# Per-column weight scales from products on TensorE, and column scales moved into the third stage's split

## The chip, the cores and the metric

The kernel runs on one core of one Trainium2 chip. The metric is the device time of one execution in microseconds (us), lower is better. The engines are named as in the profile: PE multiplies matrices (PEld is its weight load), DVE and ACT work on vectors, POOL is GpSimd, and SP issues nearly all DMAs.

## What is computed

An attention over 4 batches of 12 heads (448 rows, head size 64, RMS-normed q and k) is followed by two MLPs on 1792 tokens. The weights arrive as 64-bit floats.

```
def _moe_ref(x, w_a, w_b, w_out):
    a = x @ w_a
    b = x @ w_b
    return (a * b @ w_out)
def _moe2_ref(x, w_in, w_out, alpha):
    h = x @ w_in
    g = np.maximum(h, 0.0) + alpha * np.minimum(h, 0.0)
    return (g @ w_out)
...
    attn_out = _attn_ref(**attn_kwargs)
    x = np.ascontiguousarray(attn_out.transpose(0, 2, 1, 3)).reshape(B * S, H * D)
    x = _moe_ref(x=x, **moe_kwargs)
    return _moe2_ref(x=x, **moe2_kwargs)
```

Here w_a and w_b are 768 x 1536, the first w_out is 1536 x 768, w_in is 768 x 2048 and the second w_out is 2048 x 768.

## The kernel before

**Precision.** Every 32-bit operand of the four matrix products is written as the sum of two 16-bit halves, after a power-of-two scale that keeps it in range; a product is then three 16-bit matmuls (hi·hi, hi·lo, lo·hi: `prod`). `power` (L111 to L121) turns a sum of squares into the scale `s` and its inverse `i`, with three small DVE operations.

**Stages.** Each batch b passes four stages: a (w_a and w_b, 24 weight units of 6 chunks), y (first w_out, 12 units of 6), h (w_in, 16 units of 6) and o (second w_out, 24 units of 4). They run in the order a0 y0 h0 o0 a1 y1 a2 h1 o1 y2 a3 h2 y3 o2 h3 o3. A unit is 18 matmuls of 448 columns on PE (12 in stage o). Attention runs ahead: batch 0's before a0 (here called the prologue), the other batches' steps between the units of the stages, by the table RATE.

**Weights.** Each of the 76 units is prepared once, for batch 0, in four steps that run ahead of the unit that PE multiplies. `w_load` (10 units ahead) brings the 64-bit numbers into one of 3 `raw` buffers. `w_convert` (8 ahead) makes 32-bit floats `wf`: one ACT operation (L631), two DVE operations (L634, L637), for stage o a third that multiplies the rows by the inverse scales of stage h's columns (L643), and then an ACT Square with a running sum (L653). `w_scale` (6 ahead) sums the squares over the partitions with a matmul against ones (the tile `tot`) and calls `power`. `w_split` (3 ahead) writes the two halves (ACT L686, DVE L687) and stores them in HBM, from where the batches 1 to 3 reload them.

**Around it.** Stage h's output g is `split` with one constant `cg` (L741, L742). Stage o ends for each of 6 column blocks with ACT (L847), four transposes on PE (L854), a DVE operation `ob` that multiplies by the batch's scale `cum` (L856), and the store. A softmax step has DVE operations on the row sums `su` (L441 in batch 0, L467 later, then a reciprocal). `prep1` computes inverse roots with 3 Newton rounds of 3 DVE operations (L261, L262, L265).

**PSUM.** `ps_s` (scores) has 2 buffers of two banks, `ps_m` (tile `p`) has 3 of one bank, and `ps_x` has a single bank (tile tag `x`), which the attention's output product, `tot` and `norm` use in turn.

**Order.** The order of each engine's instructions is set when the program is built: by a scheduler that follows the order of the code as a priority and its own costs. Each engine then runs its list in order.

## Time and profile before

| what | value |
|---|---|
| median of 3 runs | 1286.08 us (1284.34 to 1286.24) |
| the profiled execution's own time | 1286.1 us |
| its span in the trace | 1283.9 us |
| PE busy | 1177.9 us, 92% of the span |
| ACT busy | 734.5 us, 57% |
| DVE busy | 709.6 us, 55% |
| POOL busy | 9.8 us, 1% |

The stretches used below begin at the first matmul of a stage on PE: prologue 0 to 117.6 us, a0 to 231.7, y0 to 294.9, h0 to 362.8, o0 to 466, a1 to 598, y1 to 653.6; then all that is left. The profile is read by these stretches, since a share over the whole span mixes a beginning in which three engines and the DMA share the load with an end in which PE has the work almost alone.

### The profile page before, as it was taken

To read this page: it belongs to the slowest core of one execution; us is meant where nothing else is said; L and a number is where in the kernel's file an instruction comes from. 1 tells how busy PE (TensorE), PEld (TensorE's weight loads), DVE (VectorE), ACT (ScalarE), POOL (GpSimd) and SP (SyncE) were. 2 spreads that over 40 slices of the span, in tenths; PEclk is the share of its full clock that TensorE was granted. 3 is DMA by queue.
4 is the path that set the end of the run, shared out by engine and by line. 5 is a ranking of instruction groups with operands and counts; after the bars stand their busy time and mean duration, and the time that the engine had idled before them with its cause. 6 is when DMAs were issued, how large, how long until landed. Compare 5 with 4: busy or idle time off the path is not lost. (4 is left out here: it accounts for less than half of the span.)

```text
span 1283.9 us, 18197 instructions
## 1 busy us (share of the span) xinstructions
PE 1177.9 (92%) x6574; PEld 604.0 (47%) x6574; DVE 709.6 (55%) x1500; ACT 734.5 (57%) x1480; POOL 9.8 (1%) x32
## 2 busy tenths in 40 slices
PE   6897998888888889887999989999999999999998
PEld 3454544444443444443545545555555555555554
DVE  7988788879897857576545166443111351102410
ACT  7999898999886867577554256544222342212310
POOL 1000000000000000000000000000000000000000
PEclk9998998898998999997999999999999999999999
DMA  6548999999989899986865375687533333344343
GB/s 187 157 156 195 299 295 299 268 296 269 285 220 251 238 235 226 206 210 164 204 153 152 115 169 133 153 189 179 150 112 113 121 112 119 94 137 137 104 124 86
DMA packets 324489, 234.66 MB, mean 183 GB/s; under 512 B 190992, under 2 KB 297744, under 8 KB 324400
## 3 DMA queue, kind: packets, MB, share of 16 engines
q1 hardware_dynamic: 324288, 233.43, 68.9%
q8 instruction: 52, 0.85, 0.3%
q0 software_dynamic: 112, 0.07, 0.1%
q14 instruction: 37, 0.30, 0.1%
HBM read 155.79 MB, written 32.24 MB: 146 GB/s over the span
## 5 line engine op out<-in xcount | busy, mean ns | idle before, releaser
L108 PEld LDWEIGHTS <-w 128*128 128x128 f16 x4896 | 480.2, 100 | 488.8 <-issue 55.5
L108 PE MATMUL p<-x,w 128*128 128x448 f16 x1728 | 339.7, 356 | 10.1 <-ACT t L760 6.7
L108 PE MATMUL p<-g,w 128*128 128x448 f16 x1152 | 232.9, 359 | 9.9 <-DVE w L687 6.9
L108 PE MATMUL p<-y,w 128*128 128x448 f16 x1152 | 225.2, 357 | 0.0
L108 PE MATMUL p<-ab,w 128*128 128x448 f16 x864 | 170.8, 359 | 1.9 <-ACT ab L741 1.9
L108 PE MATMUL s<-kT,qT 128*64 128x448 f16 (+1 forms) x588 | 105.5, 408 | 32.4 <-ACT pf L431 24.7
L414 DVE TENSOR_REDUCE nm<-s 128x2 f32<-128x896 f32 x84 | 91.0, 1084 | 36.2 <-PE s L108 35.9
L475 DVE SCALAR_TENSOR_TENSOR p<-pf,ri,p 128x448 f16<-128x448 f32 x126 | 83.2, 680 | 37.9 <-ACT p L474 37.9
L474 ACT ACTIVATE p<-pf,ri 128x448 f16<-128x448 f32 x126 | 79.9, 662 | 31.9 <-DMA pT<-p 23.5
L431 ACT ACTIVATE pf<-s,nm,esc 128x448 f32<-128x448 f32 x126 | 90.2, 720 | 2.9 <-DVE p L475 1.5
L763 DVE SCALAR_TENSOR_TENSOR ab<-p,inv_a,t 128x448 f32<-128x448 f32 x48 | 32.6, 679 | 100.2 <-PE p L108 99.8
L847 ACT ACTIVATE t<-p,inv_o 128x448 f32<-128x448 f32 x24 | 25.6, 1066 | 102.2 <-PE p L108 102.2
L631 ACT ACTIVATE wf<-raw 128x768 f32<-128x768 f32 (+1 forms) x76 | 63.2, 835 | 28.7 <-DMA raw<-in_moe_w_out_dram 8.8
L856 DVE TENSOR_SCALAR ob<-p,cum 112x512 f32<-112x512 f32 x24 | 18.0, 749 | 107.1 <-PE p L854 56.8
L687 DVE SCALAR_TENSOR_TENSOR w<-wf,sc,w 128x768 f16<-128x768 f32 (+1 forms) x76 | 69.8, 927 | 4.0 <-ACT w L686 3.7
L766 ACT ACTIVATE junk<-ab 128x448 bf16<-128x448 f32 x48 | 27.5, 573 | 74.9 <-DVE ab L763 74.1
L833 DVE SCALAR_TENSOR_TENSOR t<-t,al,p 128x448 f32<-128x448 f32 x64 | 43.4, 679 | 47.6 <-ACT t L832 47.6
L637 DVE SCALAR_TENSOR_TENSOR wf<-raw,wf 128x768 int32<-128x768 int32 (+1 forms) x76 | 65.8, 868 | 0.4
L832 ACT ACTIVATE t<-p 128x448 f32<-128x448 f32 x64 | 34.6, 541 | 54.3 <-PE p L108 54.1
L686 ACT ACTIVATE w<-wf,sc 128x768 f16<-128x768 f32 (+1 forms) x76 | 64.5, 862 | 0.3 <-DVE sc L118 0.3
L653 ACT ACTIVATE junk<-wf 128x768 bf16<-128x768 f32 (+1 forms) x76 | 59.0, 776 | 8.5 <-DVE wf L643 2.9
L741 ACT ACTIVATE g<-t,cg 128x448 f16<-128x448 f32 x64 | 42.6, 666 | 34.7 <-DVE t L833 34.6
(131 smaller groups left out, 1003.3 us busy)
## 6 DMA issues: line engine op xcount, KB each, us to landing
w<-sc_a SPq DMA_DIRECT2D x72, 384.0 KB, 3.2
w<-sc_h SPq DMA_DIRECT2D x48, 384.0 KB, 3.1
w<-sc_o SPq DMA_DIRECT2D x72, 256.0 KB, 3.1
w<-sc_y SPq DMA_DIRECT2D x36, 384.0 KB, 3.2
raw<-in_moe_w_in_dram SPq DMA_DIRECT2D x16, 768.0 KB, 7.0
raw<-in_moe_w_out_dram SPq DMA_DIRECT2D x24, 512.0 KB, 5.0
raw<-in_moe_w_a_dram SPq DMA_DIRECT2D x12, 768.0 KB, 7.2
raw<-in_moe_w_b_dram SPq DMA_DIRECT2D x12, 768.0 KB, 6.0
```

Source lines behind the costliest of these rows:

```text
L108: nc.tensor.matmul(out=o, lhsT=a, rhs=b, start=first, stop=last)
L414: nc.vector.tensor_reduce(out=nm, in_=ps[:, :, 0:S], axis=AX.X, op=ALU.max, negate=True)
L431: nc.scalar.activation(out=pf, in_=ps[:, j, 0:S], func=AF.Exp, bias=nm[:, j:j + 1], scale=scale[j], accum_out=su[:, j:j + 1],)
L474: nc.scalar.activation(out=t[:, 0, :, 0:KP], in_=pf, func=AF.Copy, scale=r)
L475: nc.vector.scalar_tensor_tensor(out=t[:, 1, :, 0:KP], in0=pf, scalar=r, in1=t[:, 0, :, 0:KP], op0=ALU.mult, op1=ALU.subtract,)
L631: nc.scalar.activation(out=t, in_=hi.bitcast(F32), func=AF.Prelu, scale=2.0 ** -112, alpha=-(2.0 ** 32))
L637: nc.vector.scalar_tensor_tensor(out=ti, in0=lo, scalar=29, in1=ti, op0=ALU.logical_shift_right, op1=ALU.bitwise_or)
L653: nc.scalar.activation(out=junk(768, size(kind)), in_=t, func=AF.Square, accum_out=sums[0][:, j:j + 1])
L686: nc.scalar.activation(out=w[:, 0], in_=t, func=AF.Copy, scale=s)
L687: nc.vector.scalar_tensor_tensor(out=w[:, 1], in0=t, scalar=s, in1=w[:, 0], op0=ALU.mult, op1=ALU.subtract)
L741: nc.scalar.activation(out=x[:, 0], in_=t, func=AF.Copy, scale=s)
L833: nc.vector.scalar_tensor_tensor(out=t, in0=t, scalar=al[:, f:f + 1], in1=ps, op0=ALU.mult, op1=ALU.add)
```

## The change

1. `w_gram` takes the place of the Square (L653). For each unit it multiplies the upper 16 bits of `wf` (read as bf16, every second 16-bit element) with themselves on PE: 6 (stage o: 4) matmuls of 128 x 128 into one tile `gram` of `ps_x`. A DVE maximum over its 128 columns gives the bound that the squares gave. It runs 6 units ahead; `w_scale` moves from 6 to 5 ahead.
2. The multiplication of stage o's rows by the inverse scales (L643) goes. `h_scales` folds these scales into a table `cgf`, one column for each f, which the split of g uses in place of `cg`. Until the table is there (in h0), g is kept as 32-bit in `raw`, and is split two at a time afterwards, the rest behind the loop.
3. `ob` moves from DVE to ACT. The third operation of `power`, the operation on `su`, the Newton rounds of all groups from the fourth on (now 4 operations in a round, on DVE as well for the first ones), and two small operations on `al` and `icg` move to POOL. The four operations on `cum` move from the end of stage y to the start of stage o.

```diff
@@ power
-        nc.vector.tensor_scalar(i.bitcast(I32), h, 1.0, float(49 << 23), op0=ALU.mult, op1=ALU.add)
+        nc.gpsimd.tensor_scalar(i.bitcast(I32), h, 1.0, float(49 << 23), op0=ALU.mult, op1=ALU.add)
@@ prep1
+        eng = nc.vector if gs[0] < 3 else nc.gpsimd
         for _ in range(3):
...
+            eng.tensor_tensor(t, r, r, op=ALU.mult)
+            eng.tensor_tensor(t, t, m, op=ALU.mult)
+            eng.tensor_scalar(t, t, -0.5, 1.5, op0=ALU.mult, op1=ALU.add)
+            eng.tensor_tensor(r, r, t, op=ALU.mult)
@@ probs (and the same in probs_f)
-        nc.vector.tensor_scalar(su, su, 1e-9, 2.0 ** -14, op0=ALU.add, op1=ALU.mult)
+        nc.gpsimd.tensor_scalar(su, su, 1e-9, 2.0 ** -14, op0=ALU.add, op1=ALU.mult)
         nc.vector.reciprocal(ri, su)
@@ w_convert, w_gram
-        if kind == "o":
-            k = CHAINS["o"][2]
-            t3 = t.rearrange("p (k f) -> p k f", f=128)
-            nc.vector.tensor_tensor(
...
+    def w_gram(u):
...
+        k = CHAINS[kind][2]
+        tops = wf[u].bitcast(BF16).rearrange("p (k f t) -> p k f t", f=128, t=2)[:, :, :, 1]
+        ps = ps_x.tile([128, 512], F32, tag="x", name="gram")[:, 0:128]
+        for kk in range(k):
+            mm(ps, tops[:, kk], tops[:, kk], kk == 0, kk == k - 1)
+        nc.vector.tensor_reduce(out=sums[0][:, j:j + 1], in_=ps, axis=AX.X, op=ALU.max)
@@ w_scale
+        if (kind, n) == ("h", KF2 - 1):
+            h_scales()
+
+    def h_scales():
+
+        mx = sm_p.tile([128, 1], F32, tag="mh", name="mh")
+        ci = sm_p.tile([128, 1], F32, tag="mh", name="ci")
+        nc.vector.tensor_reduce(out=mx, in_=inv["h"], axis=AX.X, op=ALU.max)
+        nc.vector.tensor_scalar(
+            ci.bitcast(I32), mx.bitcast(I32), -1.0, float(254 << 23), op0=ALU.mult, op1=ALU.add
+        )
+        nc.vector.tensor_scalar(cgf, inv["h"], ci, cg, op0=ALU.mult, op1=ALU.mult)
+        nc.gpsimd.tensor_tensor(icg, icg, mx, op=ALU.mult)
+        state["cgf"] = True
@@ steps
-    STEPS = [(w_load, 10), (w_convert, 8), (w_scale, 6), (w_split, 3)]
+    STEPS = [(w_load, 10), (w_convert, 8), (w_gram, 6), (w_scale, 5), (w_split, 3)]
@@ stage_h
+        def one(f):
+            t = raw.pop(f)
+            G[b, f] = x = slot(f"g{b}_{f}")
+            nc.scalar.activation(out=x[:, 0], in_=t, func=AF.Copy, scale=cgf[:, f:f + 1])
...
-            t = tmp()
+            raw[f] = t = tmp() if state["cgf"] else slot32(f"g32_{b}_{f}")
...
-            G[b, f] = split(t, cg, f"g{b}_{f}")
+            if state["cgf"]:
+                for x in sorted({f, min(raw)}):
+                    one(x)
+        for x in sorted(raw):
+            one(x)
@@ stage_o
-            nc.vector.tensor_scalar(ob, po, cum[:PT, b:b + 1], None, op0=ALU.mult)
+            nc.scalar.activation(out=ob, in_=po, func=AF.Copy, scale=cum[:PT, b:b + 1])
```

Of the 76 units' products, 6 stand in the prologue, 24 in a0, 12 in y0, 16 in h0 (10 of six matmuls, 6 of four) and 18 in o0 (of four). The rest of PE's order is the same in both programs.

On PE at the end of a0, before: two sums over partitions (`tot`), then the first matmuls of y0 on three units (`w16`).

```order
L108 MATMUL s_2813<-kT_2240,qT_2237 64x448
L108 MATMUL tot_2587<-ssab_130,ones_119 128x12
L108 MATMUL tot_2698<-ss_2471,ones_119 128x2
L108 LDWEIGHTS w16_2437
L108 MATMUL p_2634<-ab0_0_2595,w16_2437 128x448
L108 LDWEIGHTS w16_2579
L108 MATMUL p_2710<-ab0_0_2595,w16_2579 128x448
L108 LDWEIGHTS w16_2706
L108 MATMUL p_2812<-ab0_0_2595,w16_2706 128x448
```

The same place after (the last matmuls of one unit's `gram`, and the first of the next).

```order
L109 LDWEIGHTS wf_2643
L109 MATMUL gram_2849<-wf_2643 128x128
L109 MATMUL tot_2858<-ss_2647,ones_119 128x2
L109 LDWEIGHTS w16_2613
L109 MATMUL p_2822<-ab0_0_2783,w16_2613 128x448
L109 LDWEIGHTS wf_2755
L109 MATMUL gram_2898<-wf_2755 128x128
```

`gram`, `tot` and the next `gram` now follow each other within a few matmuls, and all of them use the one bank of `ps_x`.

On DVE in a0, before: the halves (L687) and the conversions (L634, L637) of the weights, one sum over partitions being read (L115, L118, L121), a product of the stage (`ab`), and parts of a Newton chain (L261, L262).

```order
L687 SCALAR_TENSOR_TENSOR w_1839<-wf,sc,w_1839 128x768
L637 SCALAR_TENSOR_TENSOR wf<-raw,wf 128x768
L687 SCALAR_TENSOR_TENSOR w_1880<-wf,sc,w_1880 128x768
L634 TENSOR_SCALAR wf<-wf 128x768
L261 TENSOR_TENSOR t<-r 128x30
L383 SCALAR_TENSOR_TENSOR v_1964<-vr,sx,v_1964 112x8x64
L637 SCALAR_TENSOR_TENSOR wf<-raw,wf 128x768
L634 TENSOR_SCALAR wf<-wf 128x768
L262 SCALAR_TENSOR_TENSOR t<-t,m 128x30
L687 SCALAR_TENSOR_TENSOR w_1917<-wf,sc,w_1917 128x768
L115 TENSOR_SCALAR pw<-tot 128x2
L763 SCALAR_TENSOR_TENSOR ab_0_4_1884<-p,inv_a,t 128x448
```

DVE in a0 after, around one sum over partitions.

```order
L702 SCALAR_TENSOR_TENSOR w_1853<-wf,sc,w_1853 128x768
L656 TENSOR_REDUCE ss<-gram 128x1
L778 SCALAR_TENSOR_TENSOR ab_0_2_1807<-p,inv_a,t 128x448
L633 TENSOR_SCALAR wf<-wf 128x768
L259 TENSOR_SCALAR t<-m 128x30
L633 TENSOR_SCALAR wf<-wf 128x768
L636 SCALAR_TENSOR_TENSOR wf<-raw,wf 128x768 x2
L656 TENSOR_REDUCE ss<-gram 128x1
L260 TENSOR_SCALAR r<-t 128x30
L467 RECIPROCAL ri<-su 128x2
L116 TENSOR_SCALAR pw<-tot 128x2
```

Two reads of `gram` stand among the conversions, the second two short operations ahead of the read of `tot`; the Newton rounds are gone from DVE's list, and the reciprocal of `su` now follows an operation on POOL.

On POOL in a0 after: the row sums (L466), the inverse scales (L122) and a Newton round (L263 to L266). Before, POOL had only the operations on `cum` there.

```order
L466 TENSOR_SCALAR su<-su 128x2
L122 TENSOR_SCALAR inv_a<-pw 128x2 x2
L466 TENSOR_SCALAR su<-su 128x2
L263 TENSOR_TENSOR t<-r 128x30
L264 TENSOR_TENSOR t<-t,m 128x30
L265 TENSOR_SCALAR t<-t 128x30
L266 TENSOR_TENSOR r<-r,t 128x30
L122 TENSOR_SCALAR inv_a<-pw 128x2
```

The three kinds of work stand in one list there, each behind the one ahead of it.

## Rows read from the trace of the kernel before

**Rows 1.** The page's busy table: busy us (share of the span) x instructions.

```profile
PE 1177.9 (92%) x6574; PEld 604.0 (47%) x6574; DVE 709.6 (55%) x1500; ACT 734.5 (57%) x1480; POOL 9.8 (1%) x32
```

**Rows 2.** Stretches: length, busy us (instructions) of PE, PEld, DVE, ACT, POOL; PEclk, DMA, GB/s.

```profile
0.00:117.60 117.60, 91.16 (x552) 53.25 (x553) 99.12 (x301) 103.64 (x229) 5.68 (x16) 0.94 0.62 168
117.60:231.70 114.10, 101.19 (x559) 51.17 (x558) 95.88 (x196) 100.89 (x199) 0.95 (x1) 0.96 1.03 289
231.70:294.90 63.20, 54.02 (x296) 27.07 (x296) 52.97 (x103) 58.57 (x112) 0.84 (x3) 0.91 1.08 282
294.90:362.80 67.90, 63.44 (x343) 32.28 (x342) 62.24 (x124) 57.83 (x110) 0.00 (x0) 0.95 0.96 275
362.80:466.00 103.20, 84.70 (x466) 39.71 (x464) 89.50 (x198) 80.90 (x173) 0.00 (x0) 0.93 0.92 236
466.00:598.00 132.00, 111.35 (x665) 54.48 (x664) 84.58 (x180) 83.22 (x189) 0.19 (x1) 0.95 0.91 212
...
880.00:1284.00 404.00, 396.48 (x2138) 207.06 (x2135) 86.70 (x140) 104.00 (x179) 1.34 (x7) 1.00 0.41 118
```

**Rows 3.** DVE's waits in a0: total us, times, longest.

```profile
DVE wf L634 <- ACT wf L631: 12.3, 9, 5.3
```

**Rows 4.** SP's own waits in a0, same columns.

```profile
SPq L615 <- DVE wf L637: 19.3, 9, 3.4
```

**Rows 5.** PE's waits over the whole span, same columns.

```profile
PE p L108 <- DVE w L687: 6.9, 5, 2.2
```

**Rows 6.** Groups by line and shape: busy us, mean ns | idle before, releasers.

```profile
L108 PEld LDWEIGHTS <-w 128*128 128x128 f16 x4896 | 480.2, 100 | 488.8 <-issue 55.5 <-DVE w L687 9.5 <-ACT w L686 4.3
...
L459 ACT COPY pT<-p 112x512 f32<-112x512 f32 x42 | 23.4, 613 | 3.1 <-PE p L451 2.3 <-PE x L108 0.9
...
L856 DVE TENSOR_SCALAR ob<-p,cum 112x512 f32<-112x512 f32 x24 | 18.0, 749 | 107.1 <-PE p L854 56.8 <-DMA w<-sc_o 35.3 <-DMA w<-sc_h 8.8
...
L643 DVE TENSOR_TENSOR wf<-wf,inv_h 128x512 f32<-128x512 f32 x24 | 16.3, 684 | 0.0
...
L467 DVE TENSOR_SCALAR su<-su 128x2 f32<-128x2 f32 x63 | 10.4, 165 | 48.1 <-ACT pf L431 47.8
...
L262 DVE SCALAR_TENSOR_TENSOR t<-t,m 128x30 f32<-128x30 f32 x33 | 6.2, 188 | 0.6
...
L810 DVE TENSOR_REDUCE mx<-norm 128x1 f32<-128x448 f32 x4 | 2.5, 623 | 51.9 <-PE norm L108 51.9
...
L813 POOL TENSOR_TENSOR cum<-ix,iab 128x1 f32<-128x1 f32 x4 | 1.5, 380 | 698.9 <-DVE su L467 302.8 <-DVE pw L115 221.2 <-DVE iab L121 174.9
...
L131 DVE TENSOR_REDUCE tots<-tot 128x1 f32<-128x4 f32 x6 | 0.9, 157 | 4.9 <-PE tot L108 4.9
...
L815 POOL TENSOR_TENSOR cum<-cum,icg 128x1 f32<-128x1 f32 x4 | 0.8, 190 | 0.3
```

**Rows 7.** Timeline of PE: start us, us, engine, line, operation, count.

```profile
98.73 1.04 PE L451 MATMUL p<-ident,pf 128*112 128x128 f32 x8
...
135.40 0.28 PE L108 MATMUL tot<-ss,ones 128*128 128x2 f32 x2
...
344.70 10.39 PE L108 MATMUL p<-y,w 128*128 128x448 f16 x54
```

**Rows 8.** Timeline of DVE in a0, same columns.

```profile
139.96 0.15 DVE L115 TENSOR_SCALAR pw<-tot 128x2 int32<-128x2 int32 x1
```

**Rows 9.** ACT's line 653 by stretch: length, busy us (instructions); PEclk, DMA, GB/s.

```profile
0.00:117.60 117.60, 8.72 (x18) 0.94 0.62 168
117.60:231.70 114.10, 22.35 (x48) 0.96 1.03 289
231.70:294.90 63.20, 10.24 (x22) 0.91 1.08 282
294.90:362.80 67.90, 11.77 (x28) 0.95 0.96 275
362.80:466.00 103.20, 12.94 (x36) 0.93 0.92 236
```

More of the change, by code (lines that the diff above doesn't have):

```diff
@@ L94, in attention_gated_mlps_kernel @@
     icg = const.tile([128, 1], F32, name="icg")
+    cgf = const.tile([128, KF2], F32, name="cgf")
     ssv = const.tile([KP, B, NP], F32, name="ssv")
@@ L191, in setup4 @@
         nc.vector.tensor_scalar(cg, cg, 2.0 ** -31, None, op0=ALU.mult)
-        nc.vector.tensor_scalar(al, al, -1.0, 1.0, op0=ALU.mult, op1=ALU.add)
-        nc.vector.tensor_scalar(icg, icg, 2.0 ** 31, None, op0=ALU.mult)
+        nc.gpsimd.tensor_scalar(al, al, -1.0, 1.0, op0=ALU.mult, op1=ALU.add)
+        nc.gpsimd.tensor_scalar(icg, icg, 2.0 ** 31, None, op0=ALU.mult)
     P = [dict() for _ in range(B * NP)]
@@ L259, in prep1 @@
         nc.vector.tensor_scalar(ri, ti, -1.0, float(0x5F3759DF), op0=ALU.mult, op1=ALU.add)
+        eng = nc.vector if gs[0] < 3 else nc.gpsimd
         for _ in range(3):
-            nc.vector.tensor_tensor(t, r, r, op=ALU.mult)
-            nc.vector.scalar_tensor_tensor(
-                out=t, in0=t, scalar=-0.5, in1=m, op0=ALU.mult, op1=ALU.mult
-            )
-            nc.vector.scalar_tensor_tensor(
-                out=r, in0=t, scalar=1.5, in1=r, op0=ALU.add, op1=ALU.mult
-            )
+            eng.tensor_tensor(t, r, r, op=ALU.mult)
+            eng.tensor_tensor(t, t, m, op=ALU.mult)
+            eng.tensor_scalar(t, t, -0.5, 1.5, op0=ALU.mult, op1=ALU.add)
+            eng.tensor_tensor(r, r, t, op=ALU.mult)
     def prep2f(g):
@@ L440, in probs_f @@
         ri = sm_p.tile([128, 2], F32, tag="ri", name="ri")
-        nc.vector.tensor_scalar(su, su, 1e-9, None, op0=ALU.add)
+        nc.gpsimd.tensor_scalar(su, su, 1e-9, 1.0, op0=ALU.add, op1=ALU.mult)
         nc.vector.reciprocal(ri, su)
@@ L527, in pv_out @@
         P[g] = None
-    state = dict(pin=True)
+    state = dict(pin=True, cgf=False)
     preps = (prep2, prep3, prep4)
@@ L639, in w_convert @@
         )
-        if kind == "o":
-            k = CHAINS["o"][2]
-            t3 = t.rearrange("p (k f) -> p k f", f=128)
-            nc.vector.tensor_tensor(
-                t3, t3,
-                inv["h"][:, part * k:(part + 1) * k].unsqueeze(2).to_broadcast([128, k, 128]),
-                op=ALU.mult,
-            )
         wf[u] = t
+    def w_gram(u):
+        if u not in wf:
+            return
+        kind, n, part = stream[u]
         _, parts, _ = CHAINS[kind]
@@ L652, in w_convert @@
             sums[0] = sm_p.tile([128, 4], F32, tag="ss", name="ss")
-        nc.scalar.activation(
-            out=junk(768, size(kind)), in_=t, func=AF.Square, accum_out=sums[0][:, j:j + 1]
-        )
+        k = CHAINS[kind][2]
[4 more added lines that the diff above has]
+        nc.vector.tensor_reduce(out=sums[0][:, j:j + 1], in_=ps, axis=AX.X, op=ALU.max)
         if j == parts * GROUP[kind] - 1:
@@ L823, in stage_h @@
     def stage_h(b):
+        raw = {}
+        def one(f):
+            t = raw.pop(f)
+            G[b, f] = x = slot(f"g{b}_{f}")
+            nc.scalar.activation(out=x[:, 0], in_=t, func=AF.Copy, scale=cgf[:, f:f + 1])
+            nc.vector.scalar_tensor_tensor(
+                out=x[:, 1], in0=t, scalar=cgf[:, f:f + 1], in1=x[:, 0],
+                op0=ALU.mult, op1=ALU.subtract,
+            )
         for f in range(KF2):
@@ L860, in finish @@
             )
+        c = cum[:, b:b + 1]
+        nc.gpsimd.tensor_tensor(c, ix[:, b:b + 1], iab[:, b:b + 1], op=ALU.mult)
+        nc.gpsimd.tensor_tensor(c, c, iy[:, b:b + 1], op=ALU.mult)
+        nc.gpsimd.tensor_tensor(c, c, icg, op=ALU.mult)
+        nc.gpsimd.tensor_tensor(c, c, ix[:, b:b + 1], op=ALU.mult)
         late = None
```

5 lines of the change are left out of this document (removed).

## Prediction

> **What bounds the kernel now.** The sum is made against the profiled execution's own 1286.1 us, of which its span is 1283.9 us; the median of the three runs is 1286.08 us, so nothing has to be converted. The first view is the page's busy table: PE is busy for 92% of the span and no other engine comes near [rows 1]. A reader who stops there would say that any new matmul costs its full time. The second view corrects that. Cut into stages, PE is idle for 7.5 of the 404 us after 880, but for 26.4 us in the prologue, 12.9 in a0, 9.2 in y0, 4.5 in h0, 18.5 in o0 and 20.7 in a1 (length less busy time), at a granted clock of 0.91 to 0.96 where the end has 1.00 [rows 2]. In the first five of these stretches, 466 us in which all weights are prepared, PE is busy for 394.5 us, DVE for 399.7 and ACT for 401.8: three engines at 85%, with the DMA engines at a share near 1 from a0 on. Nothing is saturated alone, they pass work round. DVE's shifts wait 12.3 us for ACT's conversion in a0 [rows 3], SP holds back the next raw load 19.3 us until DVE has freed a buffer [rows 4], and PE waits for DVE's weight halves [rows 5]. In a0 PE is not the slow one: a sum over partitions ended on PE at 135.68, and DVE, working through its list, read it at 139.96, 4.3 us later [rows 7, 8].
>
> So the change is judged in these 466 us: it takes work from ACT and DVE and gives some to PE.
>
> **The parts. ACT** loses all of line 653: 8.7, 22.4, 10.2, 11.8 and 12.9 us in the five stretches, 66.0 together [rows 9]. It gains 24 `ob`. A copy of the same shape out of PSUM takes ACT 613 ns, DVE takes 749 for `ob` [rows 6]; I take 0.61 us, 3 us of it in o0 (5 of the 24), the rest where ACT is at 26% [rows 2]. At the very end this saves 0.1 us.
>
> **DVE** gains 76 maxima over 128 columns. A reduction of 4 columns takes 157 ns and one of 448 takes 623 [rows 6]; on the line between them 128 columns cost 0.29 us, 22 us in all. It loses 18 row multiplications of 0.684 us in o0 and 6 in h0 (16.4), 5 `ob` in o0 (3.7), 45 operations on `su` of 0.165 (7.4), some 38 third operations of `power` at about the same price (6), and 5 Newton chains of 9 operations of 0.188 us (8.5) [rows 6]. The four chains that stay get 12 more operations (2). Net in the 466 us: 22 + 2 - 42 = -18 us. `h_scales` is three small operations once, at 0.16 each: 0.5 us beside other work. After the change ACT has 339 us there and DVE 382.
>
> **PE** gains 408 matmuls of 128 columns, each with a new load. From below: 54 matmuls of 448 columns take 10.39 us, 0.192 each, so 128 columns at that rate are 0.055 us. From above: 8 transposes of 32-bit 128 x 128 take 1.04 us, 0.13 each [rows 7]. I take 0.10, the mean of a weight load [rows 6], because a matmul that is shorter than its load cannot hide it. That is 0.6 us for a unit of six and 0.4 for one of four: 3.6 us in the prologue (6 units), 14.4 in a0 (24), 7.2 in y0 (12), 8.4 in h0 (10 and 6), 7.2 in o0 (18), 40.8 in all; at the ends 22 and 53. The operand steps over every second 16-bit element; no row shows such a load. The Trainium skill, page "TensorE: Matmul & The Clock Gate", section "Back-to-back issue gap", gives about 81 ns for each load and matmul of 128 columns in a stream; by that the 408 are an estimated 33 us, 8 less than I take, and the forecast would be some 5 us lower. No run here shows it yet.
>
> **POOL** gets the rest: 84 `su`, 45 inverse scales, 10 Newton chains of 12. Its small operations take 190 to 380 ns [rows 6], so a chain is 2.3 to 4.6 us in place of 1.7. Behind it in POOL's list stand the row sums, for which DVE's reciprocal waits, and behind that the probabilities on DVE. The scheduler has moved the consumers back, so I book nothing for most of it, and up to 0.4 us for each of the 21 softmax steps of the prologue if that cover is gone. The Trainium skill, page "GPSIMD Engine Reference", section "Specifications", says that POOL shares its SBUF interfaces with VectorE and is held up by DVE instructions with two SBUF inputs, of which this kernel has many; no row shows it, and it would only push these prices up.
>
> **New waits.** `ps_x` has one bank. In a0 a sum over partitions now stands three to seven matmuls behind the next unit's products, and cannot start before DVE has read their maximum. Queued behind it on PE are the unit's matmuls. Before, a sum had two units (some 7 us) of room. There are 32 such sums.
>
> **Stretch by stretch:**
> - Prologue: ACT is the fullest engine (103.6 of 117.6) and goes to 95, DVE to 95, PE has room. -5 us; ends -9 (all of line 653) and +2 (the POOL hop exposed at 21 x 0.4, less the relief of 6 that is left).
> - a0: PE 101.2 + 14.4 = 115.6 us of 114.1, while ACT falls to 79. PE becomes the bound: +2; ends -6 (products at 0.055, in the idle time) and +9 (0.13 each, and waits).
> - y0: PE 54.0 + 7.2 = 61.2 of 63.2: -1 (-4 to +4).
> - h0: PE 63.4 + 8.4 = 71.8 of 67.9; four deferred splits of g behind the loop are covered by the first part of o0, which doesn't need them: +3 (-1 to +8).
> - o0: DVE is the fullest (89.5 of 103.2) and loses 12.3 + 3.7 + 1.8 + 1.7 + 0.9, gains 5.2: 74. PE 84.7 + 7.2 = 91.9 becomes the bound, with some waits 94: -9 (-14 to +2).
> - From a1 on: PE's list is the same; Newton chains and `su` over POOL against 12 us less on DVE: 0 (-4 to +6).
>
> Sum: -5 + 2 - 1 + 3 - 9 = -10, so **1276 us**.
>
> **The rivals.**
> *A, slower: the single bank ties PE to DVE.* Place: each of the 32 sums in a0 to o0 and the prologue. DVE reads late today (4.3 us in the row above), which costs nothing as long as PE has other banks to fill; behind the change PE must wait for it. For: the lag, and DVE still at 82%. Against: with ACT relieved DVE should lag less, and PE's waiting is lost only where DVE then has nothing to do. At 0.8 us lost for each sum it is 26 us: 1276 + 26 = 1302. It turns the sign from 10 / 32 = 0.31 us for each sum.
> *B, no change: the ring of raw buffers and the DMA set the pace.* For: DMA share near 1, and SP's waits. Then a lighter ACT only waits longer; o0 gains 1 in place of 9, y0 nothing: -5 + 2 + 0 + 3 - 1 = -1, 1285 us. Against: SP waits for DVE there, and not for a landing.
> *C, the full relief.* The products cost 0.055 us and fall into PE's idle time: -8 - 5 - 4 + 0 - 14 = -31, 1255 us. Against: it needs no new wait at all.
> That the change doesn't do what it says is excluded by its order: line 653 and the row multiplication are gone, 76 products are there.
>
> **How the numbers follow.** Forecast 0.48, A 0.26, B 0.13, C 0.13. The range goes from 1254, which takes in C, to 1299, which leaves out the worse half of A. A measurement of this kernel tells 0.2% (2.6 us) from no change. Faster by more: the forecast but for its upper edge (0.46), C (0.13) and a little of B (0.01), 0.60. Same: most of B and that edge, 0.13. Slower: A and what is left, 0.27.
>
> **What would show it.** In the trace after: o0 10% shorter with DVE near 74 us; ACT's conversions no longer awaited by DVE in a0; the products at 0.5 to 0.6 us a unit; PE waiting before `tot` for the maximum by less than 0.3 us each. Wrong if those waits add up to more than 10 us in a0 to h0 (A), if o0 keeps its length (B), or if the later stages, whose order is unchanged, move by more than 6 us.

## The result, and the profile after

The changed kernel takes 1302.07 us (median of 5 runs, 1294.54 to 1304.26), the kernel before 1286.08 beside it: a ratio of 1.012, 95% interval 1.0084 to 1.0156. It is slower by 1.2% (some 15 us), where 1276 us was forecast, and it lies above the forecast's range. The number of rival A, 1302, was hit; whether its mechanism was, the experiments had to show.

The profiled execution took 1304.3 us, the slowest of the five. Its busy table answers to [rows 1]:

```profile
PE 1206.7 (93%) x6982; PEld 629.2 (48%) x6982; DVE 672.9 (52%) x1322; ACT 696.8 (54%) x1352; POOL 82.1 (6%) x284
```

The work moved as the diff says: DVE lost 37 us, ACT 38, POOL gained 72 and PE 29. Stretches of the changed kernel, prologue to a1, with the columns of [rows 2] (length, busy us of PE, PEld, DVE, ACT, POOL; granted clock, DMA share, GB/s):

```profile
0.00:121.10 121.10, 94.73 (x586) 56.05 (x587) 94.75 (x266) 96.04 (x211) 20.16 (x68) 0.96 0.58 163
121.10:241.90 120.80, 112.63 (x708) 60.20 (x706) 102.82 (x198) 87.24 (x154) 16.69 (x45) 0.96 0.99 290
241.90:308.30 66.40, 60.40 (x377) 32.26 (x376) 58.51 (x113) 52.95 (x96) 5.65 (x14) 0.94 1.04 274
308.30:381.60 73.30, 68.78 (x415) 36.45 (x414) 61.64 (x121) 47.01 (x81) 3.92 (x13) 0.96 0.89 246
381.60:481.10 99.50, 85.10 (x543) 43.46 (x541) 73.92 (x158) 69.57 (x136) 8.87 (x27) 0.97 0.93 245
481.10:613.90 132.80, 111.37 (x661) 54.36 (x658) 76.80 (x136) 83.02 (x190) 12.83 (x53) 0.95 0.87 196
```

Against [rows 2] the prologue is 3.5 us longer, a0 6.7, y0 3.2, h0 5.4 and a1 0.8; o0 is 3.7 shorter; behind a1 the two differ by 2.5 us in 686. In a0 ACT fell from 100.9 to 87.2 us, where 79 was forecast, and PE rose from 101.2 to 112.6. What PE waited for over the whole span (us in total, times, longest):

```profile
PE tot L109 <- DVE ss L656: 16.6, 10, 3.9
PE s L109 <- ACT pf L430: 13.0, 9, 3.9
PE p L320 <- DVE kd L273: 7.5, 2, 4.1
```

The first of these is what rival A had in mind; 12.7 us of it fall in a0 to h0, more than the 10 that the prediction named as the sign of A. One case in a0, on PE's timeline and then on DVE's (start us, us, engine, line, operation, count, idle before):

```profile
152.97 0.51 PE L109 MATMUL gram<-wf 128*128 128x128 bf16 x6
153.32 0.73 PE L109 MATMUL p<-x,w 128*128 128x448 f16 x3
157.90 0.59 PE L109 MATMUL tot<-ss,ones 128*128 128x2 f32 x2 [3.85 <-DVE ss L656]
```

```profile
156.69 0.95 DVE L636 SCALAR_TENSOR_TENSOR wf<-raw,wf 128x768 int32<-128x768 int32 x1
157.56 0.28 DVE L656 TENSOR_REDUCE ss<-gram 128x1 f32<-128x128 f32 x1
```

The products of a unit end at 153.48, DVE takes their maximum at 157.56, 4.1 us later. It is the lag of [rows 8], and now PE stands for 3.85 us of it. That a wait is there doesn't yet say that it sets the time.

And what DVE waits for at POOL, over the whole span of the changed kernel:

```profile
DVE ri L467 <- POOL su L466: 64.1, 38, 2.5
...
DVE qr L327 <- POOL r L266: 23.2, 8, 3.9
...
DVE ri L441 <- POOL su L440: 6.2, 9, 1.2
...
DVE kd L273 <- POOL r L266: 2.5, 1, 2.5
```

By size the row sums' scaling `su` (70 us) looks three times as dear as the Newton chains (`r`, 26 us). The experiments don't bear that order out.

### The profile page after: what moved, and what is told of

It reads as the page before. It is cut to its first block, busy times and chain, and to the rows that moved or that the text cites. A ratio compares the mean times of both kernels' runs of the same rounds, so it can differ in the third digit from the quotient of the medians.

```text
span 1302.4 us, 18954 instructions
## 1 busy us (share of the span) xinstructions
PE 1206.7 (93%) x6982; PEld 629.2 (48%) x6982; DVE 672.9 (52%) x1322; ACT 696.8 (54%) x1352; POOL 82.1 (6%) x284
## 4 chain that ended last, share of the span: by engine, by line
PE 49%; ACT 2%; issue 1%; DMA 1%; DVE 1%; SPq 1%; POOL 0%; ACTq 0%; POOLq 0%
PE p L109 45%; PE s L109 1%; PE x L109 1%; PE p L879 1%; ACT pf L430 1%; DMA pT<-p 1%; DVE nm L413 0%; PE norm L109 0%; DMA kr<-in_k_dram 0%; ACT p L473 0%; DMA kT<-k 0%; SPq L480 0%; ACT t L872 0%; SPq L354 0%; SPq L351 0%
## 5 line engine op out<-in xcount | busy, mean ns | idle before, releaser
L109 PE MATMUL p<-g,w 128*128 128x448 f16 x1152 | 229.7, 354 | 3.7 <-ACT w L701 3.3
L109 PE MATMUL s<-kT,qT 128*64 128x448 f16 (+1 forms) x588 | 110.1, 410 | 14.4 <-ACT pf L430 13.0
L854 DVE SCALAR_TENSOR_TENSOR t<-t,al,p 128x448 f32<-128x448 f32 x54 | 36.7, 679 | 100.1 <-ACT t L853 99.9
L853 ACT ACTIVATE t<-p 128x448 f32<-128x448 f32 x54 | 29.2, 541 | 55.4 <-PE p L109 55.3
L839 ACT ACTIVATE g<-t,cgf 128x448 f16<-128x448 f32 x54 | 36.0, 667 | 36.7 <-DVE t L854 36.7
L775 ACT ACTIVATE t<-p,inv_a 128x448 f32<-128x448 f32 x48 | 30.2, 629 | 43.7 <-PE p L109 43.5
L840 DVE SCALAR_TENSOR_TENSOR g<-t,cgf,g 128x448 f16<-128x448 f32 x54 | 36.9, 682 | 30.9 <-ACT g L839 30.9
```

What stands on the lines that cost most here:

```text
L109: nc.tensor.matmul(out=o, lhsT=a, rhs=b, start=first, stop=last)
L839: nc.scalar.activation(out=x[:, 0], in_=t, func=AF.Copy, scale=cgf[:, f:f + 1])
L840: nc.vector.scalar_tensor_tensor(out=x[:, 1], in0=t, scalar=cgf[:, f:f + 1], in1=x[:, 0], op0=ALU.mult, op1=ALU.subtract,)
L854: nc.vector.scalar_tensor_tensor(out=t, in0=t, scalar=al[:, f:f + 1], in1=ps, op0=ALU.mult, op1=ALU.add)
```

## The experiments

All were timed in 5 rounds against the kernel before on the same chip, where that took 1284.6 to 1286.2 us. "Median" is what the expectations below speak of; "us" is the ratio less one, times 1285; an interval of 0.2% is 2.6 us. The lengths are those of the profiled execution, one for each kernel, and the scheduler orders each kernel anew: split_only is 2.3 us shorter than the kernel before in prologue and a0, which its edit doesn't touch, so differences of that size in a length prove little. Prologue and a0 stand together, because a0 is counted from its first product, which a shorter prologue can place ahead of work that then falls into a0.

| kernel | median | ratio (95%) | us | prologue + a0 | y0 + h0 | o0 | a1 |
|---|---|---|---|---|---|---|---|
| before | | | | 231.7 | 131.1 | 103.2 | 132.0 |
| after | 1302.1 | 1.0120 (1.0084 to 1.0156) | +15 | 241.9 | 139.7 | 99.5 | 132.8 |
| split_only | 1274.9 | 0.9937 (0.9913 to 0.9961) | -8 | 229.4 | 127.2 | 97.9 | 129.9 |
| no_pool | 1285.6 | 1.0012 (0.9996 to 1.0028) | +2 | 236.8 | 132.0 | 96.9 | 131.5 |
| no_gram | 1284.5 | 0.9996 (0.9983 to 1.0008) | -1 | 234.3 | 135.6 | 93.9 | 133.6 |
| gram_ps_m | 1302.8 | 1.0149 (1.0129 to 1.0170) | +19 | 247.2 | 135.3 | 95.6 | 133.8 |
| pe_products | 1288.0 | 1.0008 (0.9990 to 1.0026) | +1 | 237.6 | 132.5 | 94.3 | 132.0 |
| dve_maxima | 1285.4 | 0.9998 (0.9980 to 1.0017) | 0 | 227.3 | 139.5 | 95.7 | 131.9 |
| early_maxima | 1265.6 | 0.9848 (0.9829 to 0.9867) | -20 | 219.4 | 130.6 | 96.5 | 131.1 |
| early_products | 1285.6 | 0.9997 (0.9982 to 1.0013) | 0 | 239.3 | 138.8 | 91.1 | 129.1 |
| su_pool | 1273.4 | 0.9908 (0.9889 to 0.9926) | -12 | 225.9 | 135.4 | 96.5 | 127.5 |
| newton_pool | 1293.0 | 1.0061 (1.0040 to 1.0081) | +8 | 235.5 | 135.6 | 99.0 | 134.5 |
| newton4_dve | 1275.6 | 0.9926 (0.9902 to 0.9950) | -10 | 235.2 | 135.5 | 94.0 | 130.5 |
| newton_late | 1278.7 | 0.9943 (0.9921 to 0.9966) | -7 | 228.0 | 131.6 | 97.6 | 134.0 |
| newton_back | 1285.8 | 0.9990 (0.9973 to 1.0007) | -1 | 234.4 | 136.4 | 99.0 | 128.0 |
| after_three_op_head | 1292.3 | 1.0075 (1.0050 to 1.0100) | +10 | 233.4 | 137.1 | 97.5 | 133.1 |
| after_four_op_dve | 1288.1 | 1.0023 (1.0002 to 1.0045) | +3 | 236.3 | 135.4 | 96.9 | 129.0 |
| more_dma | 1315.8 | 1.0250 (1.0224 to 1.0275) | +32 | 253.3 | 143.3 | 98.0 | 133.6 |
| su_pool_products_8 | 1272.2 | 0.9904 (0.9886 to 0.9923) | -12 | 225.1 | 131.7 | 98.6 | 132.0 |
| su_pool_scale_7 | 1275.8 | 0.9926 (0.9898 to 0.9954) | -10 | 224.2 | 138.4 | 94.5 | 130.8 |

newton4_dve's profiled execution was the slowest of its six (1282.1 us at a median of 1275.6); its lengths are not typical of it.

**The three parts taken apart.** The theories were H, that the hops to GpSimd cost the time, and A, that the single `ps_x` bank does.

no_pool puts the small operations back on VectorE:

```diff
-        nc.gpsimd.tensor_scalar(su, su, 1e-9, 1.0, op0=ALU.add, op1=ALU.mult)
+        nc.vector.tensor_scalar(su, su, 1e-9, None, op0=ALU.add)
...
-        eng = nc.vector if gs[0] < 3 else nc.gpsimd
```

> The changed kernel with all small operations that went to GpSimd (row sums' scaling, the Newton chains, inverse scales, two set-up operations) back on VectorE as before; products on PE, the column split of g and ob on ACT stay. Theory H (the hops DVE to POOL to DVE stand on the path: 64 us of DVE waits behind the row-sum operation, 23 behind the Newton chains, and the prologue's late restart): most of the 18 us goes, 1278 to 1284 us, and the prologue falls back from 121 to 115 us or less. Theory A (the one ps_x bank ties PE to DVE's maxima): the products are all still there, so 1298 to 1306 us, prologue about 119.

no_gram puts the squares back on ACT and leaves the small operations on GpSimd:

```diff
-        for kk in range(k):
-            mm(ps, tops[:, kk], tops[:, kk], kk == 0, kk == k - 1)
-        nc.vector.tensor_reduce(out=sums[0][:, j:j + 1], in_=ps, axis=AX.X, op=ALU.max)
+        nc.scalar.activation(
+            out=junk(768, size(kind)), in_=t, func=AF.Square, accum_out=sums[0][:, j:j + 1]
+        )
```

> The changed kernel with ACT's sum of squares back in place of the products on PE (at the old place in the list of steps); small operations stay on GpSimd, the column split of g and ob on ACT stay. Theory H: the loss stays, 1293 to 1300 us, prologue 121 us or more. Theory A: the single bank is free again, so 1274 to 1282 us, with the gain in o0 (some 9 us) kept and a0, y0, h0 back at 114, 63 and 68 us.

split_only makes both edits, so that the column scales in g's split (with the operations on `cum` and `icg` that go with them) and `ob` on ACT are all that is left of the change:

```diff
-            G[b, f] = split(t, cg, f"g{b}_{f}")
+            if state["cgf"]:
+                for x in sorted({f, min(raw)}):
+                    one(x)
...
-            nc.vector.tensor_scalar(ob, po, cum[:PT, b:b + 1], None, op0=ALU.mult)
+            nc.scalar.activation(out=ob, in_=po, func=AF.Copy, scale=cum[:PT, b:b + 1])
```

> The kernel before with nothing but the third stage's column scales in its own split and ob on ACT; no products, nothing moved to GpSimd. Both theories: o0 loses 18 row multiplications of 0.684 us and 5 ob of 0.749 us on VectorE, which bounds it there, so 6 to 10 us of the 103.2 go in o0 and 0 to +3 come in h0: 1277 to 1284 us. If the products were needed for the gain in o0, then 1284 to 1288.

gram_ps_m gives the products another bank:

```diff
-        ps = ps_x.tile([128, 512], F32, tag="x", name="gram")[:, 0:128]
+        ps = new_ps()[:, 0:128]
```

> The changed kernel, with one edit: the products take a bank of the pool of three that the other matmuls use, in place of the single ps_x bank that the sums over partitions need. Theory H: the hops are unchanged, 1298 to 1305 us. Theory A: the sums no longer wait for the read of the next unit's maximum; at 0.3 to 0.8 us for each of 32 sums 10 to 26 us come back, 1278 to 1292 us.

The column split alone gains 8 us (10 between the medians), a little more than either theory expected: it was a good change. Products on top of it cost 10 (no_pool), the small operations on GpSimd on top of it 8 (no_gram), both 23. So H and A each fell as the whole cause: no_pool (1285.6) and no_gram (1284.5) lie outside the ranges of both. The wait that A named doesn't set the time by itself either: in gram_ps_m no sum waits for a maximum any more, the 16.6 us of the first wait above are gone, and the time is not shorter. These are the longest of PE's waits that gram_ps_m has instead, whole span:

```profile
PE p L109 <- DVE ab L778: 13.1, 5, 5.1
PE s L109 <- ACT pf L430: 11.9, 10, 3.9
PE x L109 <- DVE tots L132: 9.1, 2, 5.7
```

In the changed kernel `p<-ab` had 6.5 us. PE waits as long, at other places. This doesn't clear the banks as such: the products now take one of the three banks of the ordinary products, and `p` waits 4.0 us for a maximum there. Products in a bank that nothing else uses were not tried.

**What the products cost.** pe_products adds the products to split_only and leaves the squares on ACT; nothing reads the products:

```diff
+    def w_gram(u):
...
+        for kk in range(k):
+            mm(ps, tops[:, kk], tops[:, kk], kk == 0, kk == k - 1)
...
+    STEPS = [(w_load, 10), (w_convert, 8), (w_gram, 6), (w_scale, 6), (w_split, 3)]
```

> split_only plus the 408 products on PE into the ps_x bank, whose result nothing reads: the sum of squares stays on ACT, no maxima on VectorE. Measured so far: products with maxima in place of squares cost 10.7 us over split_only, 11 of them in a0, -3.5 in the prologue. Theory P (PE's own time is on the path in a0, and its idle time there is not filled): a0 about 111.4 + 8 to 13 us, the whole 1285 to 1295 us. Theory D (it is VectorE's maxima and the reading of them): a0 at 111 to 114 us, the whole 1275 to 1279.

dve_maxima is the reverse, no_pool without the products:

```diff
-        nc.vector.tensor_reduce(out=sums[0][:, j:j + 1], in_=ps, axis=AX.X, op=ALU.max)
+        nc.vector.tensor_reduce(out=sums[0][:, j:j + 1], in_=wf[u][:, 0:128], axis=AX.X, op=ALU.max)
```

> no_pool without the products on PE: the maximum over 128 columns is taken from the converted weights themselves, so the scale bound is not that of the reference's columns (this part of the computation is left out); squares gone from ACT, maxima on VectorE. Theory P: a0 at 108 to 113 us, prologue 114 to 115, the whole 1268 to 1274 us. Theory D: a0 at 118 to 122 us, the whole 1280 to 1286.

Each costs about as much over split_only (9 and 8 us) as both together (10), which neither theory had. In prologue and a0 they do differ as theory P says: 237.6 us with the products, 227.3 with the maxima alone, 229.4 with neither; but dve_maxima then loses 12 us against split_only in y0 and h0. The edit had moved a third thing: the sum over partitions, from six units ahead of its use to five. So both forms were run with the step before it one unit earlier:

```diff
-    STEPS = [(w_load, 10), (w_convert, 8), (w_gram, 6), (w_scale, 5), (w_split, 3)]
+    STEPS = [(w_load, 10), (w_convert, 8), (w_gram, 7), (w_scale, 6), (w_split, 3)]
```

> no_pool with the products one unit earlier (seven units ahead in place of six) and the sums over partitions where they were in the kernel before (six ahead in place of five). Theory P (PE's own time for the products is on the path, about 9 us in prologue and a0): 1282 to 1288 us, a prologue and a0 of 235 to 238 us together. Theory O (the sum over partitions now stands only two units ahead of the split that waits for its scale, and directly behind the products): 1272 to 1279 us, and PE's waits before the sums, 6.2 us in a0, under 2 us.

> dve_maxima with the maxima one unit earlier and the sums where they were in the kernel before (seven and six units ahead). As there, the maxima are taken from the weights themselves and not from products, so that part of the computation is left out. Theory W (the shorter way from the sum to the split costs the 12 us that dve_maxima lost in y0 and h0 over split_only): 1270 to 1276 us. Theory M (moving 66 us of ACT's squares to 22 us on VectorE costs by itself, as VectorE is the fuller engine there): 1282 to 1288.

early_products (1285.6) came out as theory P had it, early_maxima (1265.6) below both of its ranges. The pair has the same steps at the same places, as many maxima on VectorE and no squares on ACT; its programs differ by the products alone (and by the order that the scheduler then makes): 20 us between the medians (1265.6 and 1285.6), and 20 us in prologue and a0 (219.4 and 239.3). Behind a0 the products cost another 8 us in y0 and h0, and 5 and 2 come back in o0 and a1. But the price holds at this distance only:

| median, us | sum five units ahead, as in the changed kernel | six units ahead |
|---|---|---|
| with the products | 1285.6 (no_pool) | 1285.6 (early_products) |
| maxima alone | 1285.4 (dve_maxima) | 1265.6 (early_maxima) |

None of the four has the small operations on GpSimd. At the changed kernel's distance the products cost 2 us, with an interval of some 3. So either one, the products or the shorter way from the sum to the split, takes back the same 20 us, and to undo one of the two gains nothing. Through which wait the shorter way does it is not shown.

Stretch a0 of early_maxima, then of early_products:

```profile
113.60:219.40 105.80, 98.57 (x558) 50.69 (x557) 99.38 (x218) 83.28 (x148) 0.64 (x1) 0.98 1.07 300
```

```profile
113.50:239.20 125.70, 112.88 (x712) 60.49 (x710) 105.00 (x223) 85.56 (x150) 0.19 (x1) 0.95 1.01 284
```

PE is busy for 14.3 us more, and its idle time does not shrink by a single one: 7.2 without the products, 12.8 with them. PE's waits in the two stretches, early_maxima's longest, then early_products' two longest:

```profile
PE tot L109 <- DVE ss L654: 5.3, 2, 3.5
```

```profile
PE tot L109 <- DVE ss L658: 9.9, 8, 3.0
PE gram L109 <- DVE ss L658: 1.9, 2, 1.5
```

Nearly all of the 12.8 us is a sum or the next product at the one bank of `ps_x`, behind a maximum that DVE reads late. So of the 20 us some 6 are rival A's kind of wait, and the rest is PE's own work. Groups of PE's instructions in the same two stretches (busy us, mean ns | idle before): early_maxima's products of x, then early_products' products of x and of the weights' columns.

```profile
L109 PE MATMUL p<-x,w 128*128 128x448 f16 x432 | 86.0, 357 | 0.0
```

```profile
L109 PE MATMUL p<-x,w 128*128 128x448 f16 x432 | 91.4, 363 | 0.0
L109 PE MATMUL gram<-wf 128*128 128x128 bf16 x156 | 13.8, 225 | 2.7 <-DVE ss L658 1.9 <-DVE pw L116 0.6 <-DVE sc L119 0.3
```

These busy times overlap, since the end of a group is still counted when the next matmul has begun: 13.8 and the 5.4 that the products of x gained are more than the 14.3 in all. Counted from each matmul's start to the next one's, without idle time, the 156 products take 10.2 us (65 ns each), the 432 products of x 3.2 us more than in early_maxima, and the rest 0.9. A part of those 3.2 us is the clock. PE around one of its waits in early_products, and the stretches on both sides of the clock's return (columns as above, the third number from the end is the granted clock):

```profile
139.39 0.58 PE L109 MATMUL tot<-ss,ones 128*128 128x2 f32 x2 [3.00 <-DVE ss L658]
139.84 4.80 PE L109 MATMUL p<-x,w 128*128 128x448 f16 x13
...
145.79 3.58 PE L109 MATMUL p<-x,w 128*128 128x448 f16 x18
```

```profile
137.46:144.28 6.82, 4.89 (x15) 2.22 (x16) 5.97 (x16) 3.49 (x7) 0.00 (x0) 0.50 1.05 234
144.28:178.42 34.14, 31.16 (x206) 17.12 (x205) 29.81 (x66) 24.42 (x42) 0.00 (x0) 1.00 1.01 289
```

At a granted clock of 0.50, the lower level of 1.2 GHz, 13 products of x take 4.80 us, 0.37 each; at 1.00 18 take 3.58 us, 0.20 each. The clock fell at 137.46, while PE stood 3.00 us for a maximum. In early_products' a0 22 products of x begin at the lower level, in early_maxima's 9: some 2 us.

more_dma was to ask whether the transfers hold the pace, so that idle time of PE can't be filled:

```diff
         raws[u] = t
+        more = hbm.tile([128, 2, 128], I64, name=f"more{u}")
+        nc.sync.dma_start(out=more, in_=source(*key)[:, 0:2])
```

> The changed kernel with 262 KB more moved for each of the 76 weight units, DRAM to DRAM, from SP's queue beside the raw load; nothing reads it. In a0 to o0 some 275 GB/s are moved at a DMA share near 1. Theory B (the transfers set the pace there): 20 MB more at that rate is 70 us, so 1340 to 1375 us. Theory P (the engines set it, and the transfers have room): 1300 to 1312 us, with a higher rate of bytes in a0.

20 MB more cost 16.6 us between the ratios. Both expectations missed, P's narrowly. But the added transfers did not stand beside their raw loads: nothing in the program holds them there, and most went into the prologue. When they were issued (durations of the issue in ns, first and last start in us):

```profile
L619 SPq DMA_DIRECT2D more<-in_moe_w_in_dram x16: 542/614/1362, 73.0 to 95.6; - x16
L619 SPq DMA_DIRECT2D more<-in_moe_w_a_dram x12: 542/607/1088, 7.3 to 59.3; - x12
L619 SPq DMA_DIRECT2D more<-in_moe_w_b_dram x12: 543/609/817, 8.0 to 59.9; - x12
```

The 40 for the stages a and h were all issued before a0 begins at 124.8 us; the other 36 run from 60.5 to 391.9, with none between 121.1 and 264.1. Prologue and a0:

```profile
0.00:124.80 124.80, 94.80 (x586) 55.57 (x587) 94.49 (x266) 96.13 (x212) 19.68 (x68) 0.95 0.90 272
124.80:253.30 128.50, 113.24 (x714) 60.51 (x713) 104.30 (x196) 87.00 (x156) 12.00 (x33) 0.96 0.94 279
```

Of the 20 MB 14.2 were moved in the prologue, at 272 GB/s in place of 163 and with 3.7 us more, so there the transfers had much room. In a0 only 0.7 MB were added, and why a0 is 7.7 us longer is not shown. So the run doesn't test whether the transfers set the pace in a0. What can be said is that they don't make the difference of the pair above: early_products moves 284 GB/s in its a0, early_maxima 300. Whether 300 is a limit remains open.

**Which of the small operations.** Each group alone on top of split_only:

```diff
-        nc.vector.tensor_scalar(su, su, 1e-9, None, op0=ALU.add)
+        nc.gpsimd.tensor_scalar(su, su, 1e-9, 1.0, op0=ALU.add, op1=ALU.mult)
```

> split_only plus only the 84 scalings of the row sums on GpSimd, between ACT's exponentials and VectorE's reciprocal. All POOL moves together cost 9.5 us over split_only, 5.8 of them in the prologue. Theory Hs (the hop in the softmax steps): prologue 121 to 124 us, the whole 1280 to 1285. Theory Hn (the Newton chains): no more than 2 us, 1273 to 1277.

```diff
+        eng = nc.vector if gs[0] < 3 else nc.gpsimd
...
-            nc.vector.tensor_tensor(t, r, r, op=ALU.mult)
+            eng.tensor_tensor(t, r, r, op=ALU.mult)
```

> split_only plus only the Newton chains in four operations for each step, the first calls on VectorE and the ten later ones on GpSimd. Theory Hn (12 more operations for each of VectorE's chains at the head of the prologue, and 2.3 to 4.6 us chains on GpSimd): prologue 121 to 124 us, the whole 1280 to 1285. Theory Hs: no more than 2 us, 1273 to 1277.

su_pool costs nothing (-12 against -8 us, intervals that touch), though in it DVE waits for POOL as long as in the changed kernel (whole span of su_pool):

```profile
DVE ri L469 <- POOL su L468: 63.6, 37, 2.2
```

newton_pool costs 16 us, and its 1293.0 lies above both ranges. Its two halves, alone on split_only: the chains in four operations a step, but all on VectorE; and the ten later chains on GpSimd, with the first four on VectorE in three operations.

```diff
-            nc.vector.scalar_tensor_tensor(
-                out=t, in0=t, scalar=-0.5, in1=m, op0=ALU.mult, op1=ALU.mult
-            )
+            nc.vector.tensor_tensor(t, t, m, op=ALU.mult)
+            nc.vector.tensor_scalar(t, t, -0.5, 1.5, op0=ALU.mult, op1=ALU.add)
```

> split_only with the Newton chains written in four operations for each step, all on VectorE; nothing on GpSimd. newton_pool, in which ten of the chains were on GpSimd as well, was 18 us above split_only. Theory F (the four kept chains at the head of the prologue, with three more operations of some 0.2 us each step on a chain of dependent operations, and what the scheduler then puts where): 1288 to 1294 us, with a prologue of 121 to 124. Theory L (the later chains on GpSimd, 12 operations each and a handover on both sides): 1274 to 1279 us.

```diff
+            if gs[0] < 3:
...
+                continue
+            nc.gpsimd.tensor_tensor(t, r, r, op=ALU.mult)
+            nc.gpsimd.tensor_tensor(t, t, m, op=ALU.mult)
```

> split_only with the ten later Newton chains on GpSimd in four operations a step, the first four on VectorE in the old three. Theory F: 1274 to 1279 us, prologue 116 to 119. Theory L: 1288 to 1294 us.

Neither half alone costs anything that these runs can tell from nothing (-1 and +1 us over split_only, each within some 4). Each theory blamed one half, so both fell: the cost is in the combination. The same on the changed kernel: first all chains back to VectorE in three operations, then only the first four, then all on VectorE in four.

```diff
-        eng = nc.vector if gs[0] < 3 else nc.gpsimd
```

> The changed kernel with one edit: all Newton chains back on VectorE in three operations a step. The products, the scalings of the row sums, the inverse scales and the two set-up operations stay as changed. If the chains are what the move to GpSimd costs, the 16 to 18 us between the changed kernel and no_pool go: 1283 to 1287 us. If another of the small operations on GpSimd has a part in it beside the products (the set-up operation on al, which held GpSimd's list for 10 us in the prologue), 1292 to 1298 us.

> The changed kernel with one edit: the first four Newton chains, which stayed on VectorE, are written in three operations a step again; the ten on GpSimd stay there. In the changed kernel all chains cost 16.3 us; on split_only the four-operation form on VectorE alone cost 0.7 and the move to GpSimd alone 3.7. Theory F (the longer chain at the head makes the first softmax step 2.5 us late and the seventh 4 to 6, and that is what the rest of the prologue does not get back): prologue 113 to 116 us, step 6 at 41 to 42, the whole 1286 to 1291. Theory L (the ten chains on GpSimd): 1298 to 1302.

> The changed kernel with all Newton chains on VectorE in four operations a step, none on GpSimd. after_three_op_head put the four chains at the head back to three operations and got 9.8 us, all in the prologue; the 6.5 us that newton_back got beside it lay in a1, where the ten chains are on GpSimd. If the two add up: 1294 to 1298 us, prologue 119 to 123 and a1 back at 128 to 130. If the handover to GpSimd has no part of its own: 1300 to 1303.

All chains back gives 17 us, and the products, `su`, the inverse scales and the set-up operations on GpSimd stay; newton_back equals no_pool (0.9990 and 1.0012), so those others together cost nothing. Three operations at the head again give 6 us by the ratios (9.8 between the medians), VectorE for all chains 12 (14). Against newton_back the ten chains on GpSimd alone (after_three_op_head) cost 11 us and the four operations alone (after_four_op_dve) 4, both together 17, with intervals of some 4 to 5: on the changed kernel they may add up, on split_only they don't. after_three_op_head (1292.3) fell between its two ranges, after_four_op_dve (1288.1) below both.

**The traces show two delays; that either one costs is not shown.** The head: PE's transposes of the third `kd` (k scaled by the chain's result) in the kernel before, in the changed one and in after_three_op_head, with the wait ahead of them in brackets.

```profile
39.33 0.57 PE L321 MATMUL p<-ident,kd 112*128 112x112 f32 x4 [1.65 <-DVE kd L274]
```

```profile
43.96 0.57 PE L320 MATMUL p<-ident,kd 112*128 112x112 f32 x4 [4.11 <-DVE kd L273]
```

```profile
39.45 0.87 PE L328 MATMUL p<-ident,kd 112*128 112x112 f32 x4 [1.86 <-DVE kd L281]
```

In PE's list the products and transposes of the running softmax steps stand behind them, and in ACT's list the exponentials of the seventh step stand behind the copy of these transposes. The first of those exponentials, in the same order:

```profile
41.34 0.74 ACT L431 ACTIVATE pf<-s,nm,r 128x448 f32<-128x448 f32 x1
```

```profile
47.56 0.72 ACT L430 ACTIVATE pf<-s,nm,r 128x448 f32<-128x448 f32 x1
```

```profile
42.54 0.73 ACT L438 ACTIVATE pf<-s,nm,r 128x448 f32<-128x448 f32 x1
```

With the longer chain at the head the seventh step starts 6.2 us late; with three operations a step there it starts 1.2 us late, and the prologue is 111.1 us in place of 121.1. But newton4_dve has the same late head, the same two lines:

```profile
43.36 0.57 PE L319 MATMUL p<-ident,kd 112*128 112x112 f32 x4 [3.89 <-DVE kd L272]
```

```profile
46.03 0.73 ACT L429 ACTIVATE pf<-s,nm,r 128x448 f32<-128x448 f32 x1
```

Its seventh step starts 4.2 us behind split_only's (41.80), and it takes no longer than split_only. So this delay alone is not what costs. The second place is the chain on POOL; its first and last operation in the prologue of the changed kernel:

```profile
66.65 0.47 POOL L263 TENSOR_TENSOR t<-r 128x30 f32<-128x30 f32 x1 [5.30 <-DVE r L260]
...
70.41 0.25 POOL L266 TENSOR_TENSOR r<-r,t 128x30 f32<-128x30 f32 x1
```

It takes 4.0 us, and DVE's wait for `qr` (23.2 us above) is for such chains; 10.1 of them fall in a1. newton_late has 26.5 us of these waits (`qr` and `kd`) and costs nothing that can be told either. In the seven kernels with ten chains on GpSimd a1 lasts 132.8 to 134.5 us, in the others 127.5 to 132.0. Why a late head and slow chains together cost more on split_only than each alone is not shown. It fits that a delay is taken up as long as the prologue's later steps have room for it; that was not tried.

**What is best.** The parts that gained, put together: the column split, `ob` on ACT and `su` on GpSimd, with products for the first eight weight units only (those converted while ACT is the fullest engine); and su_pool with the scale one unit earlier.

```diff
+    HYB = 8
...
+        if u not in wf or u >= HYB:
+            return
```

> split_only, the scalings of the row sums on GpSimd (1273.4 us with these two), and the products on PE for the first eight weight units only, which are converted in the prologue; ACT squares the other 68. If the prologue's gain from the products (3.5 us, ACT being the fullest engine there and PE having room) stands by itself: 1268 to 1271 us, prologue 108 to 110. If later stages take it back: 1273 to 1276.

```diff
-    STEPS = [(w_load, 10), (w_convert, 8), (w_scale, 6), (w_split, 3)]
+    STEPS = [(w_load, 10), (w_convert, 8), (w_scale, 7), (w_split, 3)]
```

> su_pool (column split of g, ob on ACT, row sums' scaling on GpSimd; 1273.4 us) with the sums over partitions and the scales one unit earlier, seven units ahead in place of six. Between dve_maxima and early_maxima one unit more from the sum to the split was worth 20 us. If that distance is short here too: 1262 to 1269 us. If six units are enough where nothing is put on PE: 1271 to 1276.

su_pool_products_8 takes 1272.25 us, 1.0% under the kernel before and 2.3% under the changed one; without the eight units' products (su_pool, 1273.4) it is the same within the intervals, so the prologue's gain is taken back. The earlier scale gives nothing here (1275.8 against 1273.4), as its second range had it. early_maxima is faster (1265.6) but leaves out a part of the computation, since its maxima are not the columns' bounds.

## Why the prediction was wrong, point by point

The sum was 28 us off in the profiled execution (-10 forecast, +18 measured): 8.5 in the prologue (+3.5 where -5 stood), 4.7 in a0, 4.2 in y0, 2.4 in h0, 5.3 in o0 and 3.3 behind. The experiments put this down to two steps of about equal size: products and maxima on top of split_only cost 10 us where a gain was forecast, and the operations on GpSimd another 14 (no_pool against the changed kernel) where nothing was.

**The step that failed first: "PE 101.2 + 14.4 = 115.6 us of 114.1 ... +2" in a0.** Its price was too high and its use wrong. 0.10 us for each product was taken because a load could not be hidden; 156 of them in a0 of early_products took 10.2 us from start to start, 65 ns each, while their loads are shown busy for 101 ns each. (The Trainium skill, "TensorE: Matmul & The Clock Gate", section "Back-to-back issue gap", has about 81 ns for a load and matmul of 128 columns in a stream; the trace has less.) That PE's busy time rose by 14.3 us in that pair, as if by the forecast's 14.4, is luck: the rest is other matmuls that took longer, some of it at the lower clock. Wrong was to let the added time fall into PE's 12.9 idle us of a0. PE's idle time there is 12.9 us before, 8.2 after, 7.2 and 12.8 in the last pair, 11.9 in split_only, 10.0 in no_pool and 14.3 in dve_maxima: whatever stands on PE, it waits for some 7 to 14 us of a0. Against the kernel before, prologue and a0 are 12.3 us shorter with the squares gone and nothing on PE (early_maxima), and 7.6 longer with the products (early_products); the sum had -5 and +2 for the two.

**A step priced at nothing.** The change also moves the sum over partitions from six units ahead to five. The prediction says what room a sum had before ("two units (some 7 us)"), but its sum has no term for the place one unit later. Without products that one unit is worth 20 us (dve_maxima against early_maxima); with them it is worth nothing that can be told.

**The second: the Newton chains.** "The four chains that stay get 12 more operations (2)" counted DVE's busy time, and "Newton chains and `su` over POOL against 12 us less on DVE: 0" was booked for a1 and later, with +6 at its upper end. All chains back (newton_back) gives 17 us. In the trace the third `kd` reached PE 4.6 us late, the seventh step began 6.2 us late, and a1 is 1 to 5 us longer; with three operations at the head the prologue is 111.1 us, 6.5 shorter than before, near the -5 that was forecast. But each half alone costs nothing on split_only, with the same late head or the same waits for POOL. That the chains cost it together is shown; by what path stays open.

**Right:** `su` on POOL at nothing. su_pool bears it out, with 69 us of DVE's waits in its trace; in the prologue the 0.4 us for each step did not come. The maximum took 282 ns where 0.29 us was booked; `ob` on ACT 684 ns where 0.61 was. The gain in o0 in part: DVE fell to 73.9 us (74 forecast), but the length fell by 3.7 us and not 9, and the other kernels gain 4 to 12 there (split_only 5.3, no_pool 6.3, no_gram 9.3); why the changed one gains least is not shown. h0 and y0 became longer by 5.4 and 3.2 us, where +3 and -1 were forecast; PE's added time there was 5.3 and 6.4 us, so it counted in full in h0 and by half in y0.

**The rivals.** A named the time (1302) and the wait, and its number is luck: the waits are there, 16.6 us, but newton_back keeps the single bank and is 17 us faster, and gram_ps_m without these waits is no faster. That the bank has a part is not excluded: it is where PE idles in a0 of early_products. B forecast no change and an o0 that keeps its length; the kernel is slower and o0 3.7 us shorter. C had the price of the products nearly right (0.055 us, where 0.058 to 0.065 was measured) and fell by the idle time that they could not use.
